# An attention layer and a routed expert layer on one core: token turning, early results and early weights in another order

## The chip, the core and the metric

The kernel runs on one core of a Trainium2 chip. The core has five engines that run at the same time, each with its own queue of instructions, taken in order: TensorE (PE in the profile; its weight loads are PEld) multiplies matrices, VectorE (DVE) and ScalarE (ACT) work elementwise, GpSimd (POOL) does the same more slowly and issues the transfers with computed addresses, and SyncE (SP) issues plain transfers. Engines wait for each other and for transfers (DMA) by semaphores. Products land in PSUM, eight banks of 128 partitions by 512 words; everything else lies in SBUF.

The metric is device time in microseconds (us) of one execution.

## The reference, cut to what matters

First a linear attention with a state per head, for 4 batches, 8 heads, 768 steps and 48 channels a head:

```
for t in range(S):
    cur   = u * k_t  (outer)  v_t
    y_t   = r_t . (state + cur)
    state = w * state + k_t (outer) v_t
```

Its output, 3072 tokens of 384 channels, goes through a layer of 8 experts, of which each token takes one:

```
logits     = x @ w_gate                     # 3072 x 8
expert_idx = argmax(logits); gate = softmax(logits)[expert_idx]
for e in range(8):
    h        = relu(x[mask_e] @ w1[e])      # 384 -> 1024
    out[mask_e] = gate * (h @ w2[e])        # 1024 -> 384
```

All is computed in 32-bit floats.

## The kernel before, in words

The order of the work is written out by hand: what stands first in the program stands first in its engine's queue, and nothing is moved by a scheduler.

**Attention in 16 turns.** A turn `i` is one batch and one pair of heads; time is cut into 6 chunks of 128 steps (`G = 6`). SP loads `rk` (keys and receptances) and `vk` (values and keys by token). VectorE scales the first by powers of the decay (`RK`, L257). In a turn TensorE runs, in this order: `p_own(i)` (L276, a token's product with itself, into bank `dsb`), `p_scores` for chunks 0 to 3 (L288, banks `X0`, `X1`), `p_ds(i)` (L311, the chunks' state products, into `dsb`), `p_tr(i - 2)` (L349, tokens of two turns ago turned so that a token is a row, together with their part of the logits, into bank `tr` and a corner of `X23`), `p_scores` for chunks 4 and 5 (`X23`), and `p_out(i - 1)` (L331 and L336, outputs of the turn before, into `yps`). In turns 6 and 10 and 14, between `p_ds` and `p_tr`, small products rank a batch's tokens within their experts (`p_rank`, L376 to L379). ScalarE builds diagonals (L294) from `own`, VectorE masks scores into them (L300, L302) and runs the states through time (`scan`, L316), ScalarE copies outputs (`out_t`, L341) and turned tokens (`keep`, L354 and L355, into `xb`). Two products into `dsb` or reads of it are ordered as if the whole bank were one thing: a product waits until VectorE has read what stood there before.

**Routing.** After a batch's last turn, VectorE finds each token's expert (`choose`), `slots` gives it a row in a table `rows` in memory, ordered by expert, and POOL sends tokens there, 128 at a time (`send`, L401, one indirect transfer per chunk). Of the batch before the last, chunk 0 goes in turn 14 and chunks 1 to 5 in turn 15.

**Experts.** Experts 0 and 1 start early: their first 160 tokens, known to be there after three batches, run as two `early` passes. Eight `late` passes follow: the rest of experts 0 and 1 (224 and 192 tokens), then the other six by size (416 down to 364), whose numbers are read by SP at run time. A pass has an inner layer `L1` (L463: for each of 8 blocks `f`, three products into one of four banks, then a ReLU on ScalarE, L465) and an outer layer (`L2`, L474, channels as rows, transposed by VectorE, scaled into `yo`; and `tokens_out`, L502, for the first 128 or 256 tokens, tokens as rows). Results go to `out` by indirect transfers on POOL (`scatter`, L520). Weights stand in two sets of buffers, `w1s` and `w2s`, each of four quarters of 384 KB; pass `k` uses set `k % 2`. SP loads them (`weights`, L420): `w1s(0)` in turn 12, `w2s(0)` in turn 13, `w1s(1)` in turn 14, `w2s(1)` in turn 15. SP also loads the passes' rows (`load`, L446), behind the sends that write them.

**Around the change.** In turn 12, `count(cnt2)` (a product with ones, L412, and a subtraction on VectorE, L413) tells if experts 0 and 1 have their 160 tokens. Early inner layers are mixed into the end of the attention: blocks 0 and 1 of the first pass, then `p_tr(14)`, `keep(14)`, `p_out(15)`, block 2, `p_tr(15)`, `keep(15)`, `choose(3)`, blocks 3 to 5, `p_rank(3)`, the sends of the last batch, and the rest. Then both early outer layers, and a check that all decays are in range: `in_range` (two VectorE instructions, L205 and L206, that make `okw`), a product with ones (L680, into `tr`), and the sum into `flag` (L681, L683). The late passes come after it. A kernel for inputs that break these assumptions (`general`) stands behind a branch on `flag` and doesn't run here.

A one-element copy on POOL into `turn` (L572 and others) computes nothing that is used: POOL waits for what it reads, and so does everything behind it.

Of the kernel before, what the change touches and what calls it, by code (L numbers as in the profile page):

```python
# [20 lines left out]
N = B * S  # L21
# [22 lines left out]
def straight(tc, rk, vk, w, w1, w2, out, flag):  # L44
# [365 lines left out]

    def count(dst):
        nc.tensor.matmul(dsb[:, 480:480 + E], lhsT=ones, rhs=osum, start=True, stop=True, skip_group_check=True)  # L412
        nc.vector.tensor_tensor(dst, dsb[:, 480:480 + E], basef, op=ALU.subtract)  # L413


    def weights(ws, w, k):

        e = late[k].e if k < E else k - E
        for q in range(4):
            nc.sync.dma_start(ws[k % 2][q], w[e, q] if isinstance(e, int) else w[ds(e, 1), q].rearrange("e p a c -> (e p) a c"))  # L420

    def weights1(k):
        weights(w1s, w1, k)

    def weights2(k):
        weights(w2s, w2, k)

    class Pass:
# [29 lines left out]
        def L1(self, fs=range(FT)):  # L458
            h = self.h
            for f in fs:  # L460
# [4 lines left out]
                nc.scalar.activation(h[:, f, 0:self.n], p[:, 0:self.n], func=ACT.Relu)  # L465

        def L2(self):
# [20 lines left out]
            for j in range(g):  # L488
                scatter(out4, ix[:, j:j + 1], yo[:, j, :], N * HP)
# [42 lines left out]
    for b in range(B - 1):  # L532
        for k, cs in enumerate(((0,), (1, 2), (3, 4), (5,)) if b < B - 2 else ((0,), (1, 2, 3, 4, 5))):
            sends[4 * b + 6 + k] = (b, cs)
# [30 lines left out]
    for i in range(1, U):  # L565
# [3 lines left out]
        p_own(i)  # L569
        own_t(i)  # L570
        if i > 1:
# [12 lines left out]
        mask(i, 1)  # L584
        p_ds(i)
# [4 lines left out]
        if 2 <= i:  # L590
            p_tr(i - 2)
# [20 lines left out]
        if i == 12:  # L612
            weights1(0)
            count(cnt2)
            nc.vector.tensor_scalar(out=viol[:, 12:14], in0=cnt2[:, 0:2], scalar1=float(EARLY), scalar2=None, op0=ALU.is_lt)
# [12 lines left out]
    p_out(U - 1)  # L628
    out_t(U - 1)
    early[0].L1(range(2, 3))  # L630
# [5 lines left out]
    early[0].L1(range(3, 6))  # L636
# [4 lines left out]
    early[0].L1(range(6, FT))  # L641
    early[1].L1()
# [14 lines left out]

    count(cnt)
# [14 lines left out]
    for p in late[2:]:  # L673
        p.e = nc.values_load(who[0:1, p.k - 2:p.k - 1], engines=[ENG.SP], min_val=2, max_val=E - 1,
                             skip_runtime_bounds_check_because="a sum over one place")
    early[0].L2()
    late[0].xT()
    early[1].L2()
    in_range()
    nc.tensor.matmul(tr[:, 496:496 + HP], lhsT=ones[0:KP], rhs=okw, start=True, stop=True, skip_group_check=True)  # L680
# [539 lines left out]
```

## Time and profile before

| | us |
|---|---|
| median of 4 runs | 390.74 |
| the four runs | 388.79, 390.67, 390.81, 391.04 |
| the profiled execution, its own time | 390.26 |
| its span, first to last instruction | 388.5 |
| TensorE busy | 374.8 |
| VectorE, ScalarE, POOL busy | 138.4, 121.2, 148.1 |
| turns of the attention | to 113.6 |
| early passes | 113.6 to 146.2 |
| late passes | from 148.1 |

The span is one execution; its own time is 1.76 us longer. Lines of the profile are read so: a group has the line of the kernel, the engine, the operation, `out<-in` by the program's tile names, shapes, how many, and then busy us and mean ns. A product of 32-bit floats is recorded twice, so eight products count x16. A wait reads "engine, what it was about to do `<-` whom it waited for: us in total, times, the longest". The chain follows the work that ended last back from the end: start, length, what. "issue" in it is time in which nothing that the profile shows was waited for. In a table of stretches, the five engines' busy time is followed by the granted TensorE clock (1.00 is full), the share of the DMA engines' time, and GB/s.

### The profile page before, as it was taken

The numbers are of one execution on the slowest core, as the hardware profiler recorded it, in microseconds if no ns is written. First come the engines' busy times: TensorE is split into PE (matmuls) and PEld (weight loads), VectorE is DVE, ScalarE is ACT, GpSimd is POOL, SyncE is SP. The second block draws the span as 40 slices with busy tenths as digits, with TensorE's granted clock in tenths as the row PEclk, the third lists the DMA queues.
The fourth block names the chain that finished last, engine by engine and source line by source line (L and its number), as shares of the span: only waits on it lengthen the run. The fifth ranks groups of instructions, "written<-read, shape, count | busy, mean of one in ns | idle before, by whom it ended". The sixth has DMA issues, their size and how long they took to land.

```text
span 388.5 us, 7741 instructions
## 1 busy us (share of the span) xinstructions
PE 374.8 (96%) x2997; PEld 285.0 (73%) x2997; DVE 138.4 (36%) x334; ACT 121.2 (31%) x348; POOL 148.1 (38%) x163
## 2 busy tenths in 40 slices
PE   6999999999999998999999999999999999999992
PEld 6788888888888997985585675585576567766761
DVE  8977796888852232030111121111102112111020
ACT  2678687877774201301202201210210120001100
POOL 3479689988851536003021034005105203342051
PEclk9999999999999998999999999999999999999997
DMA  7996886868689342859339317514823832502301
GB/s 217 286 255 212 260 251 220 273 186 270 218 255 384 132 90 76 199 164 283 101 96 250 112 62 203 154 54 146 228 82 101 225 96 86 173 19 89 117 21 46
DMA packets 34974, 65.00 MB, mean 167 GB/s; under 512 B 18378, under 2 KB 19410, under 8 KB 34928
## 3 DMA queue, kind: packets, MB, share of 16 engines
q1 hardware_dynamic: 31120, 54.58, 47.8%
q0 software_dynamic: 3808, 9.84, 7.0%
q8 instruction: 25, 0.41, 0.4%
q14 instruction: 21, 0.17, 0.1%
HBM read 53.29 MB, written 11.26 MB: 166 GB/s over the span
## 4 chain that ended last, share of the span: by engine, by line
PE 93%; issue 2%; DVE 1%; POOL 1%; ACT 0%; POOLq 0%
PE X L463 33%; PE tr L502 11%; PE yps L474 10%; PE dsb L502 8%; PE X L288 7%; PE yps L331 6%; PE dsb L474 5%; PE tr L349 4%; PE yps L336 3%; PE dsb L311 2%; PE X L349 2%; PE dsb L276 2%; POOL rp L263 0%; DVE pw L127 0%; DVE yps L68 0%
## 5 line engine op out<-in xcount | busy, mean ns | idle before, releaser
L463 PE MATMUL X<-xT,w1s 128*128 128x224 f32 (+7 forms) x384 | 115.5, 462 | 0.4 <-PE tr L680 0.4
L463 PEld LDWEIGHTS X<-xT,w1s 128*128 128x128 f32 x384 | 72.9, 194 | 43.3 <-issue 23.5
L465 ACT ACTIVATE hT<-X 128x224 f32<-128x224 f32 (+7 forms) x64 | 29.6, 462 | 203.1 <-PE X L463 203.1
L520 POOL DMA_INDIRECT out_dram<-yo,ix x33 | 32.3, 978 | 158.5 <-DVE ia L497 130.4
L294 ACT ACTIVATE A<-ident,own 128x128 f32<-128x128 f32 x192 | 57.9, 388 | 7.3 <-DVE own L280 7.3
L502 PE MATMUL tr<-w2s,hT 128*128 128x384 f32 x128 | 48.4, 487 | 0.0
L502 PE MATMUL dsb<-w2s,hT 128*128 128x384 f32 x96 | 37.7, 486 | 0.0
L401 POOL DMA_INDIRECT rows<-xb,slot x24 | 29.6, 1231 | 15.2 <-issue 6.4
L502 PEld LDWEIGHTS tr<-w2s,hT 128*128 128x128 f32 x128 | 23.8, 190 | 14.8
L474 PEld LDWEIGHTS yps<-hT,w2s 128*128 128x128 f32 x256 | 32.5, 191 | 2.0 <-issue 0.9
L474 PE MATMUL yps<-hT,w2s 128*128 128x96 f32 (+7 forms) x256 | 33.3, 283 | 0.0
L288 PE MATMUL X<-RK 48*128 48x128 f32 x384 | 30.3, 289 | 1.7 <-DVE RK L257 1.7
L476 DVE STREAM_TRANSPOSE yq<-yps 128x160 f32<-128x160 f32 (+3 forms) x16 | 5.1, 321 | 74.8 <-PE yps L474 74.8
L455 DVE STREAM_TRANSPOSE xT<-xs 128x416 f32<-128x416 f32 (+3 forms) x24 | 11.3, 521 | 53.3 <-DMA xs<-rows 53.2
L288 PEld LDWEIGHTS X<-RK 48*128 48x128 f32 x384 | 24.0, 187 | 8.5 <-issue 4.6
L257 DVE TENSOR_TENSOR RK<-rk,TT 112x1536 f32<-112x1536 f32 x16 | 27.7, 1731 | 0.0
L502 PEld LDWEIGHTS dsb<-w2s,hT 128*128 128x128 f32 x96 | 18.2, 190 | 12.7
L263 POOL TENSOR_TENSOR rp<-rk 112x768 f32<-112x768 f32 x15 | 27.3, 1818 | 0.1
L300 DVE COPY_PREDICATED A<-strict,X 128x512 f32<-128x512 int32 x32 | 22.9, 733 | 4.5 <-ACT A L294 4.4
L331 PE MATMUL yps<-A,vk 128*48 128x128 f32 x384 | 24.3, 276 | 0.0
L520 POOL DMA_INDIRECT out_dram<-yt,it x14 | 13.7, 978 | 25.0 <-DVE yt L514 23.1
L514 DVE TENSOR_SCALAR yt<-tr,xg 128x384 f32<-128x384 f32 x8 | 4.9, 618 | 51.1 <-PE tr L502 51.1
(134 smaller groups left out, 396.3 us busy)
## 6 DMA issues: line engine op xcount, KB each, us to landing
w1s<-in_w_dram SPq DMA_DIRECT2D x40, 384.0 KB, 3.1
w2s<-in_w_dram SPq DMA_DIRECT2D x32, 384.0 KB, 3.8
rk<-in_rk_dram SPq DMA_DIRECT2D x16, 672.0 KB, 6.8
vk<-in_vk_dram SPq DMA_DIRECT2D x16, 528.0 KB, 4.5
xs<-rows SPq DMA_DIRECT2D x16, 169.0 KB, 4.9
rows<-zt SPq DMA_DIRECT2D x1, 1248.0 KB, 6.7
xs<-rows SPq DMA_DIRECT2D x8, 156.0 KB, 4.3
out_dram<-yo,ix POOLq DMA_INDIRECT x33, 2.2
```

Of the source, the lines that this page charges most:

```text
L257: nc.vector.tensor_tensor(RKs[i % 3][0:KP].rearrange("p u (c t) -> p u c t", t=C), x[0:KP].rearrange("p u (c t) -> p u c t", t=C), bc(TT[: ...
L263: (eng or nc.gpsimd).tensor_tensor(rps[i % 2][0:KP], x[0:KP, 0], x[0:KP, 1], op=ALU.mult)
L288: nc.tensor.matmul(o, lhsT=r[q, 1, c * C:(c + 1) * C], rhs=r[q, 0, c * C:(c + 1) * C], start=True, stop=True, skip_group_check=True)
L294: nc.scalar.activation(A[:, place(c, h), :], ident, func=ACT.Copy, scale=own[i % 2][:, c, h:h + 1])
L331: nc.tensor.matmul(o(c, h), lhsT=v[:, c, h * D:(h + 1) * D], rhs=A[:, place(c, h), :], start=c < 2, stop=c == 0, skip_group_check=True)
L349: nc.tensor.matmul(trv[c // 4][:, c % 4, :], lhsT=yTs[i % 3][0:KP, c & 1, (c // 2) * C:(c // 2 + 1) * C], rhs=sel[:, c & 1, i % HP, :], st ...
L401: s_ = nc.gpsimd.indirect_dma_start(out=rows[:, :], out_offset=bass.IndirectOffsetOnAxis(ap=slot[b % 2][:, c:c + 1], axis=0), in_=xbs[b % ...
L463: nc.tensor.matmul(p[:, 0:self.n], lhsT=w1s[self.k % 2][f // 2][:, m, f % 2 * 128:(f % 2 + 1) * 128], rhs=self.t[:, m, 0:self.n], start=m ...
L465: nc.scalar.activation(h[:, f, 0:self.n], p[:, 0:self.n], func=ACT.Relu)
L474: nc.tensor.matmul(p[:, 0:n], lhsT=w2s[self.k % 2][f // 2][:, f % 2, m * 128:(m + 1) * 128], rhs=self.h[:, f, self.c:self.n], start=f == 0 ...
L502: nc.tensor.matmul(tbank[t][:, 0:DM], lhsT=self.h[:, f, t * 128:(t + 1) * 128], rhs=w2s[self.k % 2][f // 2][:, f % 2, :], start=f == 0, st ...
L520: s_ = nc.gpsimd.indirect_dma_start(out=to[:, :], out_offset=bass.IndirectOffsetOnAxis(ap=at, axis=0), in_=x, in_offset=None, bounds_check ...
```

## The change

- In each turn from 2 on, `p_tr(i - 2)` stands ahead of `p_ds(i)` (and of the ranks) instead of behind them.
- The product of `count` is split off as `p_count`. In turn 12 it stands right behind `p_own(12)`, with the subtraction and the comparison right behind `own_t(12)`.
- SP loads half of `w1s(0)` in turn 12 and the other half in turn 14. The loads of `w1s(1)`, `w2s(0)` and `w2s(1)` are issued by ScalarE, one quarter behind one ReLU of the early inner layers.
- Of batch 2, chunks 3 to 5 are sent after `keep(14)`, behind a copy into `turn`.
- `L2` of an early pass no longer scatters its results. Its ten transfers stand one at a time in the first three late inner layers, each behind a copy into `turn` that reads a finished block of `h`.
- `in_range` moves ahead of the first late transposes, and the check's product and sum (`okay`) behind the first late inner layer and the second late transposes.

```diff
-    def weights(ws, w, k):
+    def weights(ws, w, k, qs, eng):
...
-        for q in range(4):
-            nc.sync.dma_start(ws[k % 2][q], ...)
+        for q in qs:
+            eng.dma_start(ws[k % 2][q], ...)
...
-        def L1(self, fs=range(FT)):
+        def L1(self, fs=range(FT), then=()):
...
                 nc.scalar.activation(h[:, f, 0:self.n], p[:, 0:self.n], func=ACT.Relu)
+                if then:
+                    load, k, q = then.pop(0)
+                    load(k, (q,), nc.scalar)
...
-            for j in range(g):
-                scatter(out4, ix[:, j:j + 1], yo[:, j, :], N * HP)
+            if self.nt:
+                self.blocks_out()
+
+        def blocks_out(self, js=None):
+            for j in js or range(self.g - self.gc):
+                scatter(out4, self.ix[:, j:j + 1], self.yo[:, j, :], N * HP)
...
-        for k, cs in enumerate(((0,), (1, 2), (3, 4), (5,)) if b < B - 2 else ((0,), (1, 2, 3, 4, 5))):
+        for k, cs in enumerate(((0,), (1, 2), (3, 4), (5,)) if b < B - 2 else ((0,), (1, 2))):
...
         p_own(i)
+        if i == 12:
+            p_count()
         own_t(i)
+        if i == 12:
+            count(cnt2)
+            nc.vector.tensor_scalar(out=viol[:, 12:14], ...)
...
+        if 2 <= i:
+            p_tr(i - 2)
         p_ds(i)
         if rt:
             p_rank(b)
             slots(b)
         scan(i)
-        if 2 <= i:
-            p_tr(i - 2)
...
         if i == 12:
-            weights1(0)
-            count(cnt2)
-            nc.vector.tensor_scalar(out=viol[:, 12:14], ...)
+            weights1(0, (0, 1))
         if i == 13:
             for p in early:
                 p.load()
-            weights2(0)
         if i == 14:
-            weights1(1)
-        if i == 15:
-            weights2(1)
+            weights1(0, (2, 3))
 
-    early[0].L1(range(0, 2))
+    early[0].L1(range(0, 2), [(weights1, 1, 0), (weights1, 1, 1)])
     p_tr(U - 2)
     keep(U - 2)
+    nc.gpsimd.tensor_copy(turn, xbs[1][0:1, G - 1, 2, 0:1])
+    send(B - 2, range(3, G))
     p_out(U - 1)
     out_t(U - 1)
-    early[0].L1(range(2, 3))
+    early[0].L1(range(2, 3), [(weights1, 1, 2)])
...
-    early[0].L1(range(3, 6))
+    early[0].L1(range(3, 6), [(weights1, 1, 3), (weights2, 0, 0), (weights2, 0, 1)])
...
-    early[0].L1(range(6, FT))
-    early[1].L1()
+    early[0].L1(range(6, FT), [(weights2, 0, 2), (weights2, 0, 3)])
+    early[1].L1(range(0, 2))
+    early[1].L1(range(2, FT), [(weights2, 1, q) for q in range(4)])
...
+    p_count()
     count(cnt)
...
+    def okay():
+        nc.tensor.matmul(tr[:, 496:496 + HP], lhsT=ones[0:KP], rhs=okw, ...)
+        nc.vector.tensor_scalar(out=viol[:, E:E + HP], ...)
+        nc.vector.tensor_reduce(flag, viol[0:1, 0:E + HP + 2], axis=AX, op=ALU.add)
+
     early[0].L2()
+    in_range()
     late[0].xT()
     early[1].L2()
-    in_range()
-    nc.tensor.matmul(tr[:, 496:496 + HP], lhsT=ones[0:KP], rhs=okw, ...)
-    nc.vector.tensor_scalar(out=viol[:, E:E + HP], ...)
-    nc.vector.tensor_reduce(flag, viol[0:1, 0:E + HP + 2], axis=AX, op=ALU.add)
     n = len(late)
+    waiting = [(x, j) for x in early for j in range(ge)]
...
-            p.L1()
+            for f in range(FT):
+                p.L1((f,))
+                if (k < 2 and f % 2 or k == 2 and f % 4 == 1) and waiting:
+                    nc.gpsimd.tensor_copy(turn, p.h[0:1, f, 0:1])
+                    x, j = waiting.pop(0)
+                    x.blocks_out((j,))
             late[k + 1].xT()
+            if k == 0:
+                okay()
```

More of the change, by code (lines that the diff above doesn't have):

```diff
@@ L409, in ids, with p_count, weights1, weights2 @@
                        channel_multiplier=4)
+    def p_count():
+        nc.tensor.matmul(dsb[:, 480:480 + E], lhsT=ones, rhs=osum, start=True, stop=True, skip_group_check=True)
     def count(dst):
-        nc.tensor.matmul(dsb[:, 480:480 + E], lhsT=ones, rhs=osum, start=True, stop=True, skip_group_check=True)
         nc.vector.tensor_tensor(dst, dsb[:, 480:480 + E], basef, op=ALU.subtract)
-    def weights(ws, w, k):
+    def weights(ws, w, k, qs, eng):
         e = late[k].e if k < E else k - E
-        for q in range(4):
[L420 to L426, printed above, removed]
+        for q in qs:
+            eng.dma_start(ws[k % 2][q], w[e, q] if isinstance(e, int) else w[ds(e, 1), q].rearrange("e p a c -> (e p) a c"))
+    def weights1(k, qs=range(4), eng=nc.sync):
+        weights(w1s, w1, k, qs, eng)
+    def weights2(k, qs=range(4), eng=nc.sync):
+        weights(w2s, w2, k, qs, eng)
     class Pass:
@@ L456, in xT @@
                                     self.x[:, 0:self.g, 32 * m:32 * m + 32])
-        def L1(self, fs=range(FT)):
-            h = self.h
+        def L1(self, fs=range(FT), then=()):
+            h, then = self.h, list(then)
             for f in fs:
@@ L569, in straight @@
         p_own(i)
+        if i == 12:
+            p_count()
         own_t(i)
+        if i == 12:
+            count(cnt2)
+            nc.vector.tensor_scalar(out=viol[:, 12:14], in0=cnt2[:, 0:2], scalar1=float(EARLY), scalar2=None, op0=ALU.is_lt)
         if i > 1:
@@ L612, in straight @@
         if i == 12:
-            weights1(0)
-            count(cnt2)
-            nc.vector.tensor_scalar(out=viol[:, 12:14], in0=cnt2[:, 0:2], scalar1=float(EARLY), scalar2=None, op0=ALU.is_lt)
+            weights1(0, (0, 1))
         if i == 13:
@@ L675, in straight @@
                              skip_runtime_bounds_check_because="a sum over one place")
+    def okay():
+        nc.tensor.matmul(tr[:, 496:496 + HP], lhsT=ones[0:KP], rhs=okw, start=True, stop=True, skip_group_check=True)
+        nc.vector.tensor_scalar(out=viol[:, E:E + HP], in0=tr[:, 496:496 + HP], scalar1=KP - 0.5, scalar2=None, op0=ALU.is_lt)
+        with nc.allow_low_precision("whole numbers"):
+            nc.vector.tensor_reduce(flag, viol[0:1, 0:E + HP + 2], axis=AX, op=ALU.add)
     early[0].L2()
+    in_range()
     late[0].xT()
     early[1].L2()
-    in_range()
-    nc.tensor.matmul(tr[:, 496:496 + HP], lhsT=ones[0:KP], rhs=okw, start=True, stop=True, skip_group_check=True)
-    nc.vector.tensor_scalar(out=viol[:, E:E + HP], in0=tr[:, 496:496 + HP], scalar1=KP - 0.5, scalar2=None, op0=ALU.is_lt)
-    with nc.allow_low_precision("whole numbers"):
-        nc.vector.tensor_reduce(flag, viol[0:1, 0:E + HP + 2], axis=AX, op=ALU.add)
     n = len(late)
+    waiting = [(x, j) for x in early for j in range(ge)]
     for k, p in enumerate(late):
```

## The prediction

> **What bounds the kernel now.** I read the page first, then the waits of TensorE, the chain around every place where TensorE waits, and the clock there. The page's busy row says which engine to follow:
>
> ```profile
> PE 374.8 (96%) x2997; PEld 285.0 (73%) x2997; DVE 138.4 (36%) x334; ACT 121.2 (31%) x348; POOL 148.1 (38%) x163
> ```
>
> TensorE has work for 374.8 of 388.5 us, and its work is the same after the change, so time can come only from its idle places, from its clock, and from the order of its instructions. The waits name every idle place:
>
> ```profile
> PE X L288 <- DVE RK L257: 1.7, 1, 1.7
> ...
> PE X L107 <- POOL ident masks.py:199: 1.4, 1, 1.4
> ...
> PE tr L680 <- DVE okw L206: 1.4, 1, 1.4
> ...
> PE X L463 <- ACT xb L355: 0.4, 1, 0.4
> PE dsb L276 <- POOL rp L263: 0.4, 1, 0.4
> PE X L463 <- PE tr L680: 0.4, 1, 0.4
> PE dsb L276 <- DVE cnt L413: 0.4, 1, 0.4
> ```
>
> RK, ident and rp lie in the first 16 us, which the change leaves alone. Three places remain: 93.5 us (cnt), 121.5 us (xb), and the largest, where the early experts' outer layer ends and the late inner layers begin. The chain there, start and length in us:
>
> ```profile
> 143.98 2.19 PE yps L474 x16
> ...
> 146.59 0.64 DVE yoe L487
> ...
> 147.34 0.17 DVE okw L206
> ...
> 147.56 0.18 PE tr L680
> 147.74 0.35 issue
> 148.09 2.05 PE X L463 x7
> ```
>
> A tiny product (L680, the check on the decay's range) needs okw, which VectorE makes only after the second early expert's results. From 146.17 to 148.09 the array does almost nothing. The stretches that follow show a second bill; the column after the five engines' busy times is the granted clock:
>
> ```profile
> 145.60:149.00 3.40, 1.63 (x11) 1.29 (x10) 2.46 (x10) 0.00 (x0) 2.39 (x4) 1.00 0.09 29
> 149.00:152.40 3.40, 3.40 (x11) 3.08 (x10) 0.03 (x1) 0.71 (x2) 2.72 (x3) 0.50 0.12 43
> 152.40:156.00 3.60, 3.60 (x20) 3.60 (x20) 0.00 (x0) 0.99 (x3) 0.98 (x1) 0.99 0.51 160
> ```
>
> After 3.4 us in which TensorE worked only 1.63, its clock was halved for 3.4 us.
>
> **The change part by part.** *The range check.* in_range goes ahead of the first late transposes, and the L680 product behind the first late inner layer. Between L474's end and the first late L463 nothing is left: its input xT was transposed at 140.65 to 141.65, some 4.5 us early, and in_range (two instructions of 0.16) takes 0.3 of that. Gain: 148.09 - 146.17 = 1.92. The product is now paid in the middle of inner layers. Its nearest row is the other such product, L412, with 0.01 in the chain; the far end is its present 0.53 (147.56 to 148.09). I take 0.1, nearer to L412, since okw is by then long made. VectorE's answer to it queues behind the second late transposes and holds up only flag, read at the end.
>
> *The clock.* 3.4 us at half speed lose 1.7. By length: the late inner layers of width 224 and 192 took 18.80 us (148.09 to 166.89), while the one of width 416, as many columns, took 16.76 (177.41 to 194.17), a difference of 2.04, of which some is the overhead of 48 more records. I take 1.8, ends 0 (the halving comes all the same) and 2.0.
>
> [...]
>
> *The early count* (p_count, count at turn 12). Before, the next own-product waited 0.35 for cnt on VectorE (chain: L412 at 93.34, L276 at 93.81). Now the product follows p_own(12), and its 0.17 us subtraction runs beside 1.1 us of scores and 1.5 us of token turning before anything else writes dsb. Gain 0.34. On VectorE scale(13) starts some 0.35 later; RK is needed only in the next turn, over 4 us on. ScalarE's diagonals move by about 0.1, and ScalarE idles more than that in each turn.
>
> *Token turning ahead of the state products*, 14 turns. One turn before:
>
> ```profile
> 107.52 1.16 PE L288 MATMUL X<-RK 48*128 48x128 f32 x16
> 108.61 0.65 PE L311 MATMUL dsb<-vk,Kd 128*48 128x48 f32 x20
> 109.19 1.14 PE L349 MATMUL tr<-sel,yT 112*128 112x104 f32 x8
> 110.71 0.71 PE L288 MATMUL X<-RK 48*128 48x128 f32 x8
> ```
>
> By starts: scores 1.09, state products 0.58, turning 1.52, no idle. In turn 1, which has no turning, scores follow the state products at the same 0.58 (17.23 to 17.81). Near 115.36 the turning takes 1.42 ahead of L331. So the order is worth between -0.1 and +0.1 a turn, 1.4 either way in all; I take 0, because 0.58 repeats whatever follows. The state products move from 108.61 to about 110.1 and end where the turning did, at 110.71; the scan that reads them began at 111.32, behind the second mask, so it doesn't move. In turns with ranks, slots likewise waits behind masks (rko at 104.93; ranks would end near 104.2). Nor does the turning lack its input: yT was copied by 107.87, and it starts at 108.6.
>
> *Weights from ScalarE's queue.* The twelve loads of w1s(1), w2s(0), w2s(1) left SP between 107.89 and 116.30; half of w1s(0) takes their place. Now each goes out after an activation of the early inner layers. As TensorE needs f every 0.82 us and an activation takes 0.30, 0.5 us is free for an issue. Issues and landings of all sixteen before:
>
> ```profile
> L420 SPq DMA_DIRECT2D w1s<-in_w_dram x8: 430/501/1255, 92.9 to 111.3; - x8
> L420 SPq DMA_DIRECT2D w2s<-in_w_dram x8: 328/474/1318, 107.9 to 116.0; - x8
> ...
> DMA to landing us min/median/max: 3.8/9.0/11.7
> ```
>
> The median issue just fits. Before the first product of each weight there is: w1s(1) last quarter, issued about 123.4, needed at 131.2 (126.25 plus six f): 7.8 us. w2s(0) last quarter, 127.65, needed at 134.5: 6.9. w2s(1) first, 129.3, needed at 139.5: over 10. The 9.0 median would miss two of these, but it belongs to a burst of twelve loads in 8.4 us, at 396 GB/s and a DMA share of 1.02 (114 to 122 us). Spread, loads (4.7 MB) and nine sends (1.9 MB) make 6.6 MB from 115 to 136 us, 16 to 17 of 21 us at that rate; so I take 4 to 6 us, near the minimum, and no stall. One place is tight: the issue between the third activation (ends 120.47) and keep (121.05), which ends the 0.42 wait at 121.5. With 0.5 it just passes, with 1.32 it costs 0.7; I take 0.1.
>
> [...]
>
> *Sends and early results.* Three sends of batch 2 wait for keep(14) and go at about 117.4 to 121.1 instead of 112.7 to 117.6, before POOL's ids at 122.42. The last batch's sends must land before the late rows load (135.19, landing in 2.1 to 2.4); these are needed by 145, so 3 to 4 us later is still free. The ten early scatters (0.98 us each on POOL, 140.99 to 153.6) move beside the late inner layers, each behind a tiny POOL copy that waits for an activation. Behind them in POOL's order stand the late scatters, the first near 174; nothing on TensorE waits for an early scatter, and activations that reuse an h wait for a copy two passes old. Cost 0, ends 0 and 0.3 at the most, as TensorE shows no idle from 148.09 to 381.
>
> **Sum.** 1.92 - 0.1 + 1.8 + 0.34 - 0.1 = 3.9. The profiled execution took 390.26 (span 388.5 and 1.76 around it), so 386.4, span 384.6. It stands 0.5 below the median of the four runs, 390.74, which would give 386.9; I say 386.5.
>
> **Rivals.**
> *The clock's 1.8 is not won* (the halving is tied to something else): 388.3. For it: the idle 1.69 at 7.5 us shows no halving. Against: only this idle stretch fills half of 3.4 us, and the halving follows at once.
> *Half-late weights*: at 9.0 us, w1s(1)'s last quarter lands at 132.4 and w2s(0)'s at 136.65, stalling 1.2 and, since the first stall shifts the need, 1.0 more: 388.6.
> *Slower, weights late for good*: at the 11.7 us maximum they land at 135.1 and 139.35, stalls of 3.9 and 1.0, and such an idle stretch would halve the clock again, 1.7: 386.4 + 6.6 = 393.0. It decides from about 10 us on, a first stall of 2.2 with the clock's 1.7 eating the 3.9. Against it is the missing burst.
> *The turn's order*: 14 x 0.1 lost, 387.8, or gained, 385.0.
>
> **How the numbers follow.** Forecast 0.63 (own range 385.6 to 387.4); clock not won 0.08; half-late weights 0.10; slower 0.06; order lost 0.07; order gained 0.06. Up to 388.5 the range holds all but the slower case and part of two others, so 385.2 to 388.5. A measurement tells 0.5% (1.95 us) from no change: under 388.8 lies everything but the slower case and the upper parts of the second and third, so faster 0.86, same 0.09, slower 0.05.
>
> **What would show it.** Right: no TensorE wait on okw or cnt; the first late inner layer at about 145.9 directly behind L474; the two late inner layers in about 16.9 us; granted clock 1.00 until the end; turns still 6.55 us. Wrong: TensorE waiting for w1s or w2s between 124 and 140, activations lagging behind queue issues on ScalarE, a stretch of clock 0.5 elsewhere, or turns off 6.55.

## The result, and the profile after

The changed kernel took 386.75 us (median of 38 executions, 386.53 to 389.37); the kernel before, run beside it, 390.52 (median of 59, 388.40 to 393.78). The ratio is 0.9923, with a 95% interval of 0.9906 to 0.9939: faster by 0.6 to 0.9%. The medians stand 3.8 us apart, the means (387.58 and 390.61) 3.0, and the ratio lies by the means: the times of both kernels fall into groups, which are told below. The forecast was 386.5, the range 385.2 to 388.5.

The page of the changed kernel (387.4 us of span, 389.28 us of time) has the same work on TensorE, and nearly no idle place left. First its busy row, then all waits of TensorE that are named; in the second view the columns are the time waited in total, how often, and the longest.

```profile
PE 375.4 (97%) x2997; PEld 285.8 (74%) x2997; DVE 138.2 (36%) x334; ACT 121.1 (31%) x348; POOL 148.9 (38%) x174
```

```profile
PE X L288 <- DVE RK L257: 2.2, 1, 2.2
PE X L107 <- POOL ident masks.py:199: 1.4, 1, 1.4
PE X L466 <- ACT xb L355: 0.4, 1, 0.4
PE dsb L276 <- DVE rp L263: 0.2, 1, 0.2
```

Lines have moved: the inner layers' products are now L466 (L463 before), their activations L468 (L465), the outer layers' L480 (L474), the range check's product L692 (L680), the weight loads L422 (L420); L276, L288, L311, L349 stand where they stood. The waits for okw and for cnt are gone, the 0.4 for xb is as it was. The chain of the same execution at the place of the first, start and length in us:

```profile
146.30 2.17 PE yps L480 x16
148.48 9.08 PE X L466 x48
157.56 0.01 PE tr L692
157.56 7.91 PE X L466 x48
165.47 1.76 PE yps L480 x16
```

The late inner layers begin where the early outer layer ends, the check's product costs 0.01 between the two, and from the first late inner product to the first late outer one it is 16.99 us (148.31 to 165.31) in place of 18.64 (148.09 to 166.73): the granted clock is 1.00 in the one stretch and 0.91 in the other.

This execution shows something else, though, which the forecast had not foreseen. In the table of stretches, taken from one record of the clock to the next (TensorE, weight load, VectorE, ScalarE, POOL, granted clock, DMA share, GB/s) the clock is halved at the start, for twice 3.41 us:

```profile
7.98:11.39 3.41, 1.95 (x25) 1.25 (x25) 3.12 (x5) 0.38 (x2) 0.00 (x0) 1.00 1.00 270
11.39:14.80 3.41, 3.41 (x38) 2.60 (x35) 3.41 (x5) 3.41 (x13) 1.12 (x2) 0.50 1.03 257
14.80:18.22 3.42, 3.42 (x16) 3.22 (x16) 1.28 (x3) 0.25 (x1) 1.99 (x2) 0.50 1.05 292
```

It makes the stretch from the first to the second own product 8.18 us long, where the kernel before has 5.63. Among the 38 times, 25 lie between 386.5 and 387.7 and 13 between 389.0 and 389.4, a distance of 2.5: the profiled execution is one of the 13, which lie above the range. The kernel before waits for RK at its start too (1.7 us; here 2.2). So the two profiled executions of the first comparison can't simply be subtracted; the experiments below bring a pair that can.

### The profile page after: what moved, and what is told of

The parts are those of the page before. It is cut to its first block, busy times and chain, and to the rows that moved or that the text cites. A ratio compares the mean times of both kernels' runs of the same rounds, so it can differ in the third digit from the quotient of the medians.

```text
span 387.4 us, 7759 instructions
## 1 busy us (share of the span) xinstructions
PE 375.4 (97%) x2997; PEld 285.8 (74%) x2997; DVE 138.2 (36%) x334; ACT 121.1 (31%) x348; POOL 148.9 (38%) x174
## 4 chain that ended last, share of the span: by engine, by line
PE 95%; DVE 3%; issue 0%; ACT 0%; POOL 0%; POOLq 0%
PE X L466 33%; PE tr L512 11%; PE yps L480 10%; PE dsb L512 8%; PE X L288 7%; PE yps L331 6%; PE dsb L480 5%; PE tr L349 4%; PE yps L336 3%; PE dsb L311 3%; PE X L349 2%; PE dsb L276 2%; PE yps L107 1%; DVE TT L146 1%; DVE RK L257 0%; DVE pw L127 0%
## 5 line engine op out<-in xcount | busy, mean ns | idle before, releaser
L466 PE MATMUL X<-xT,w1s 128*128 128x224 f32 (+7 forms) x384 | 113.9, 457 | 0.0
L466 PEld LDWEIGHTS X<-xT,w1s 128*128 128x128 f32 x384 | 71.6, 190 | 40.9 <-issue 21.0
L468 ACT ACTIVATE hT<-X 128x224 f32<-128x224 f32 (+7 forms) x64 | 29.5, 461 | 199.4 <-PE X L466 198.7
L480 PEld LDWEIGHTS yps<-hT,w2s 128*128 128x128 f32 x256 | 32.5, 191 | 2.0 <-issue 0.9
L480 PE MATMUL yps<-hT,w2s 128*128 128x96 f32 (+7 forms) x256 | 33.3, 284 | 0.0
L288 PE MATMUL X<-RK 48*128 48x128 f32 x384 | 30.9, 293 | 2.2 <-DVE RK L257 2.2
L288 PEld LDWEIGHTS X<-RK 48*128 48x128 f32 x384 | 24.4, 190 | 7.9 <-issue 4.6
L401 POOL DMA_INDIRECT rows<-xb,slot x24 | 24.1, 1003 | 15.5 <-issue 7.0
L263 POOL TENSOR_TENSOR rp<-rk 112x768 f32<-112x768 f32 x15 | 29.4, 1958 | 0.1
```

The costliest lines, as they stand in the source:

```text
L263: (eng or nc.gpsimd).tensor_tensor(rps[i % 2][0:KP], x[0:KP, 0], x[0:KP, 1], op=ALU.mult)
L288: nc.tensor.matmul(o, lhsT=r[q, 1, c * C:(c + 1) * C], rhs=r[q, 0, c * C:(c + 1) * C], start=True, stop=True, skip_group_check=True)
L401: s_ = nc.gpsimd.indirect_dma_start(out=rows[:, :], out_offset=bass.IndirectOffsetOnAxis(ap=slot[b % 2][:, c:c + 1], axis=0), in_=xbs[b % ...
L466: nc.tensor.matmul(p[:, 0:self.n], lhsT=w1s[self.k % 2][f // 2][:, m, f % 2 * 128:(f % 2 + 1) * 128], rhs=self.t[:, m, 0:self.n], start=m ...
L480: nc.tensor.matmul(p[:, 0:n], lhsT=w2s[self.k % 2][f // 2][:, f % 2, m * 128:(m + 1) * 128], rhs=self.h[:, f, self.c:self.n], start=f == 0 ...
```

## The experiments

My theory was the sum on record: a gap behind the early outer layers (1.9), a clock halved by it (1.8), a wait for the count (0.34), and nothing from the rest. The rivals were that the clock's part comes from elsewhere, and that the other parts (turning order, weights from ScalarE's queue, early results later) are worth something after all.

The first eight kernels ran on two chips on which the kernel before took 406.92 us (17 runs, 401.16 to 410.52) and 404.99 us (11 runs, 401.69 to 411.11), some 15 more than at first. So a ratio of these eight isn't to be compared with 0.9923; what I read from them is the length of stages, which can be compared, and why these chips are slower, which is told at the end. The changed kernel itself was not run on those two chips. The last four kernels ran on a third chip, where the kernel before took 390.82 us.

**One part alone, and one part back: the range check**

To the kernel before, only this part:

```diff
     early[0].L2()
+    in_range()
     late[0].xT()
     early[1].L2()
-    in_range()
-    (product with ones, comparison, sum into flag)
 ...
             late[k + 1].xT()
+            if k == 0:
+                okay()      # the same three
```

> The kernel before with the range check alone moved (in_range ahead of the first late transposes, its product behind the first late inner layer). Theory (the wait on okw and the clock that it halves are nearly the whole gain): no TensorE wait on okw, the two late inner layers in 16.9 to 17.0 us instead of 18.8, and times in two groups, near 386.7 and 389.3, so a median some 3 us under before. Rival (the gain needs the weights or the early results out of the way): TensorE waits for something else between 140 and 150 us and the time falls by less than 1.5 us.

To the changed kernel, this part undone:

```diff
     early[0].L2()
-    in_range()
     late[0].xT()
     early[1].L2()
+    in_range()
+    okay()
 ...
-            if k == 0:
-                okay()
```

> The changed kernel with the range check back where it was. Theory: nearly all is given back: TensorE waits 1.4 us for okw again, the shortest times stand near 388.2 (386.6 and 1.9 less 0.3), the two late inner layers take 18.8 us in runs with the halved clock; median within 0.6 us of before. Rival (several parts share the gain): median at least 1.5 us under before.

By the stage: from the first product of the early outer layers to the first late inner product is 15.22 us in the kernel before (132.87 to 148.09). With the check alone moved it is 13.12 (143.63 to 156.75), in the changed kernel 13.12 (135.19 to 148.31), and with the check back 15.23 (141.94 to 157.17). So the gap is worth 2.10 us, the same by itself and put back, and the pair on the third chip below gives it too. The times were 401.49 us (397.44 to 403.19; ratio 0.986, interval 0.980 to 0.992) for the check alone and 396.23 (394.68 to 398.28; ratio 0.972, 0.967 to 0.977) for the check back. The second was expected within 0.6 us of the kernel before and is 10.7 below it: the sign that was put down for the rival, that several parts share the gain. On the slower chips other parts do have a price of their own, as the parts undone one by one show further down.

The clock is another matter. With the check back, the gap came back and the halving did not. Two stretches of that kernel, cut where the clock's records begin and end:

```profile
155.41:158.82 3.41, 1.81 (x10) 1.68 (x10) 2.36 (x10) 0.11 (x1) 0.00 (x0) 1.00 0.00 0
158.82:162.23 3.41, 3.41 (x20) 3.41 (x19) 0.00 (x0) 1.20 (x4) 1.15 (x2) 1.00 0.37 112
```

TensorE's idle 1.41 us before the product and 0.36 behind it fell so that 1.60 of them lay in the first of these stretches, with 1.81 of work; the clock stayed at 1.00. My forecast had tied the halving to the gap; the gap alone doesn't bring it. Nor does the time worked in such a stretch alone decide: in the same execution, at the early inner layers, one with 1.83 of work had a halving behind it:

```profile
117.87:121.28 3.41, 1.83 (x15) 1.50 (x14) 0.00 (x0) 1.26 (x4) 0.90 (x1) 1.00 0.51 168
121.28:124.69 3.41, 3.41 (x29) 2.87 (x27) 0.00 (x0) 0.84 (x2) 1.25 (x3) 0.50 0.53 192
```

**The gap filled, in the kernel before**

```diff
     in_range()
+    p_fill(6, X01[1][:, 0, :])
     (product with ones into tr)
```

> The kernel before with six idle products (the fill that it has at its start, 0.22 us each) ahead of the range check's product, in the time in which TensorE waits for okw. They compute nothing that is used. The wait for okw stays, only the idleness goes. Theory (the halved clock comes from the idle stretch): the two late inner layers take 16.9 us instead of 18.8 though they start no earlier (about 148.1), and the two upper groups of before's times (near 390.4 and 392.8) are gone. Rival (the halving is tied to something else there): still 18.8 us in most runs, time as before.

It took 406.1 us (400.47 to 413.72), ratio 1.0005 (0.995 to 1.006), and doesn't answer its question. The fill delayed what it was to cover: VectorE's transposes of the last early results began at 159.93, behind the end of the filling products (159.20), so the check's product still waited 2.1 us, behind the fill (159.20 to 161.30), and the clock was halved behind it:

```profile
159.59:163.01 3.42, 1.34 (x7) 1.21 (x7) 2.50 (x10) 0.00 (x0) 1.46 (x2) 1.00 0.04 14
163.01:166.42 3.41, 3.41 (x11) 3.07 (x10) 0.00 (x0) 0.71 (x2) 2.50 (x4) 0.50 0.08 29
```

What it does give is one more halving behind a stretch in which TensorE worked 1.34 of 3.42 us.

**The start filled, in the changed kernel**

```diff
-    p_fill(17, X01[1][:, 0, :])
+    p_fill(25, X01[1][:, 0, :])
```

> The changed kernel with 25 instead of 17 idle products at the start, while VectorE makes the first scaled keys. Theory (the profiled run of the changed kernel was 2.6 us longer because TensorE's idle 2.2 us at 7 us halved its clock from 11.4 to 18.2): the idle place shrinks to under 0.6 us, no run shows the halved clock there, all times lie near 386.6, and the group near 389.2 is gone. Rival (the two groups have another cause): 389.2 still shows in about a third of the runs; or the fill delays the first scores and all times rise by up to 0.5.

394.04 us (392.77 to 398.71), ratio 0.966 (0.960 to 0.972). The wait for RK at 7 us is gone and so is the halving behind it: the clock is 1.00 from 6.8 to 140.0 us, and the first own product to the second takes 5.46. The times tell nothing of the two groups on this chip, and this is one execution: that the fill removes the halving for good isn't shown by it. A halving at another place, behind a wait of 2.9 us that the executions on the third chip don't have, again follows a stretch with little work, 1.42 us:

```profile
136.54:139.95 3.41, 1.42 (x10) 1.38 (x11) 0.23 (x2) 0.90 (x3) 0.39 (x1) 1.00 1.01 405
139.95:143.37 3.42, 3.42 (x15) 3.42 (x14) 1.71 (x10) 0.01 (x1) 0.00 (x0) 0.50 0.61 203
```

**The other four parts, each undone in the changed kernel**

The turning behind the state products again:

```diff
-        if 2 <= i:
-            p_tr(i - 2)
         p_ds(i)
 ...
         scan(i)
+        if 2 <= i:
+            p_tr(i - 2)
```

> The changed kernel with the older tokens' turning back behind the state products. Theory (the order is worth nothing, as its blocks take the same time either way): turns without ranks 6.55 us as before, the three turns with ranks shorter by 0.1 (6.73 against 6.82), time within 0.4 us of the changed kernel's. Rival (the new order hides a wait): a TensorE wait for own or keys appears in some turn and the time rises by over 0.5 us.

The early weights from SP's queue again:

```diff
-            weights1(0, (0, 1))
+            weights1(0)
         if i == 13:
 ...
+            weights2(0)
         if i == 14:
-            weights1(0, (2, 3))
+            weights1(1)
+        if i == 15:
+            weights2(1)
 ...
-    early[0].L1(range(0, 2), [(weights1, 1, 0), (weights1, 1, 1)])
+    early[0].L1(range(0, 2))
     (and so at the other calls)
```

> The changed kernel with all early weights back in SyncE's queue, where they were. Theory (neither queue lets TensorE wait): time within 0.3 us of the changed kernel's; the last batch's sends land sooner, so the late rows are loaded some 3 us earlier, and TensorE doesn't notice. Rival (the saturated transfers of 114 to 122 us cost something once the check is out of the way): slower by 0.5 us or more.

The early results sent out at once again:

```diff
-            if self.nt:
-                self.blocks_out()
+            self.blocks_out()
 ...
-    waiting = [(x, j) for x in early for j in range(ge)]
+    waiting = []
```

> The changed kernel with the ten early scatters back in the early outer layers. Theory: POOL issues them at about 141 to 154 us again and nothing on TensorE changes; time within 0.3 us. Rival (ten transfers beside the late loads of rows delay the first late transposes, whose slack fell to 2.5 us): TensorE waits for xT near 146 and the time rises by 0.5 us or more.

The early count at the end of turn 12 again:

```diff
         p_own(i)
-        if i == 12:
-            p_count()
         own_t(i)
-        if i == 12:
-            count(cnt2)
-            (comparison into viol)
 ...
             weights1(0, (0, 1))
+            p_count()
+            count(cnt2)
+            (comparison into viol)
```

> The changed kernel with the early count back at the end of turn 12. Theory: TensorE waits 0.35 us for cnt again, turn 12 takes 7.1 us instead of 6.7, time up by 0.35. Rival (the wait was hidden by something): no change, under 0.1.

| undone | us (lowest, highest) | ratio to before, 95% | turns 8, 9, 10 | turns 12, 13, 14 | early inner layers |
|---|---|---|---|---|---|
| turning order | 397.32 (396.39, 399.79) | 0.984 (0.980, 0.988) | 7.47, 7.50, 7.14 | 7.26, 7.64, 7.10 | 23.75 |
| weights | 391.34 (390.03, 392.74) | 0.968 (0.964, 0.972) | 6.55, 6.55, 6.81 | 6.66, 6.77, 7.16 | 22.72 |
| early results | 394.68 (393.33, 397.76) | 0.977 (0.972, 0.982) | 6.57, 6.55, 6.81 | 6.66, 6.85, 7.13 | 25.31 |
| early count | 396.57 (393.55, 402.22) | 0.978 (0.972, 0.984) | 6.56, 6.55, 6.81 | 8.26, 6.55, 6.81 | 22.32 |

A turn is counted from the start of its own product to that of the next; the last column goes from the first early inner product to the first early outer one. From the early outer layers on, all four are alike: 13.12 or 13.13 us to the first late inner product, and 231.39 or 231.40 from there to TensorE's last product. So the early results cost the late passes nothing, sent out at once or one at a time. With the turning behind the state products, turns 8 and 9 are 0.9 us longer, 10 and 12 by 0.3 and 0.6, 13 by 0.8 to 1.1; with the count at its old place, turn 12 is 1.6 longer. On the chip of the first profiles the order was worth nothing in a plain turn but turn 3 (6.67 to 6.55) and the count 0.4, so both have a price on this chip that they don't have there. The weights have no plain reading: the early inner layers differ among these kernels by up to 3 us, in waits that come and go (and 1.7 of the 25.31 is a halved clock), and the kernel with SP's weights has 22.72, between two with ScalarE's.

**Both kernels and two variants on the third chip**

The last four ran side by side on a chip on which the kernel before took 390.82 us (17 runs): both kernels unaltered, and the changed kernel with small edits meant to be better still.

> The changed kernel unaltered, on the chip on which the kernel before is run beside it. My theory (the check's gap 1.9 to 2.1 us, the clock 1.7 only where the window of 3.4 us falls so, the count 0.4; and on a chip where TensorE's signals reach the other engines late, 0.85 us in each of several turns through the turning order and up to 2.9 us through the count): if the kernel before stands at 388 to 394 us here, this one is 2 to 5 us shorter (ratio 0.987 to 0.995) and its plain turns take 6.55 us; if the kernel before stands above 400 us, this one is 8 to 13 us shorter (ratio 0.967 to 0.98), with turns 8 to 10 at 6.55. Rival, that on such a chip everything is stretched in the same proportion and the parts of the change have the value that they have elsewhere: 3 to 5 us shorter also there (ratio 0.988 to 0.993). In either case 13.1 us from the first outer product of the first early expert to the first late inner layer.

> The kernel before unaltered, for its profile on the same chip as the others. My theory: ratio 1.0 within 0.5%; 15.2 us from the first outer product of the first early expert to the first late inner layer, with the wait of 1.9 us for okw in it, whatever the chip. On a chip where it takes over 400 us, turns 8 to 10 take 7.1 to 7.5 us each in place of 6.55, with waits between the own product and the state product, and turn 12 over 8 us; on a chip where it takes 388 to 394 us all plain turns are 6.55. Rival, stretched throughout: all turns longer by the same 3 to 4%.

The changed kernel: 386.73 us (386.56 to 386.82), ratio 0.9886 (0.985 to 0.992). The kernel before, as one of the four: 391.74 (388.61 to 392.97), ratio to itself 1.001 (0.998 to 1.005). Here neither profiled execution has a halved clock at its start, so they can be subtracted: 390.68 and 386.73 us, 3.95 between them. This execution of the kernel before has a halved clock behind the check, and not all of its executions have. Of the 29 on this chip, 9 have a mean granted clock of 0.989 to 0.991, as it has, and take 390.2 to 391.4 us; 10 have 0.993 to 0.996, as the changed kernel's six have (0.993 to 0.997), and take 388.5 to 389.9; 10 have 0.982 and take 392.7 to 393.0, which fits a start at half clock on top. So in about a third of its executions the kernel before has the gap and not the halving. The profiled kernel before, chain and stretches:

```profile
144.24 2.19 PE yps L474 x16
...
147.61 0.17 DVE okw L206
147.78 0.04 issue
147.82 0.18 PE tr L680
148.00 0.35 issue
148.35 18.80 PE X L463 x96
```

```profile
145.25:148.66 3.41, 1.64 (x12) 1.30 (x11) 1.86 (x8) 0.00 (x0) 2.70 (x3) 1.00 0.14 43
148.66:152.08 3.42, 3.42 (x11) 3.10 (x10) 0.64 (x3) 0.36 (x1) 2.50 (x4) 0.50 0.12 43
```

The changed kernel's chain there:

```profile
143.77 2.17 PE yps L480 x16
145.94 9.08 PE X L466 x48
155.02 0.01 PE tr L692
155.03 7.91 PE X L466 x48
```

And the count in turn 12, first the chain of the kernel before, then that of the changed one:

```profile
93.61 0.12 PE dsb L412
93.73 0.02 issue
93.76 0.18 DVE cnt L413
93.94 0.14 issue
94.07 0.51 PE dsb L276 x8
```

```profile
86.91 0.44 PE dsb L276 x8
87.35 0.11 PE dsb L412
87.46 1.09 PE X L288 x16
```

Before, the next own product waited for VectorE's answer; now the count's product is followed by scores at once.

The two variants were these, the second with the weights from SP's queue on top:

```diff
-    p_fill(17, X01[1][:, 0, :])
+    p_fill(25, X01[1][:, 0, :])
 ...
-        if 2 <= i:
+        if 2 <= i and not rt:
             p_tr(i - 2)
         p_ds(i)
 ...
         scan(i)
+        if 2 <= i and rt:
+            p_tr(i - 2)
 ...
-    early[0].L1(range(3, 6), [...])
+    early[0].L1((4, 3, 5), [...])
```

> The changed kernel with three small edits: 25 filling products in place of 17 at the start (they compute nothing that is used), the turning behind the state products again in the three turns with ranks alone, and the fifth inner block ahead of the fourth where the fourth waits 0.42 us for the copies of the turned tokens. My theory: no idle stretch at 7 us and so no halved clock there (2.55 us in the executions that had it), 0.3 from the turns with ranks, 0.4 from the block order: 0.7 us below the changed kernel where the clock falls well for both, 3.2 where only the changed kernel's clock is halved, so a median 0.7 to 2 us below it (ratio to the kernel before 0.002 to 0.005 lower). [...]

> The same three edits, and the early weights from SyncE's queue as in the kernel before. If issuing from ScalarE's queue costs time (the theory for a chip where the stage from the first early inner layer to the first early outer layer took 23.8 to 25.4 us with it and 22.7 without): 1 to 3 us below the kernel with the three edits alone on such a chip. If the issues run beside the activations at no cost (as in the changed kernel's profile, 0.33 us each beside activations of 0.30): within 0.3 us of it, stage 19.3 us in both.

They took 387.27 us (386.70 to 387.98; ratio 0.990, 0.987 to 0.994) and 387.10 (386.71 to 387.45; ratio 0.990, 0.986 to 0.993): neither beats the changed kernel, and the 0.7 us expected of the first didn't come. Its time is 0.5 above the changed kernel's, and no halved clock is seen that would explain it: in the profiled execution (386.70 us) the clock is 1.00 to TensorE's last product. Two of its three edits did what they were to do and found nothing to gain or gave little. None of the changed kernel's six executions here shows the 389 us of a halved start, so there was nothing for the fill to save, and whether it prevents that start isn't shown; the three turns with ranks went from 6.81 each to 6.74, 6.72 and 6.72, 0.25 in all. The third failed: with block 4 ahead of block 3, TensorE's wait for xb was replaced by a longer one. In the list of TensorE's waits the first line is of the changed kernel, the second of the variant:

```profile
PE X L466 <- ACT xb L355: 0.4, 1, 0.4
```

```profile
PE X L466 <- ACT hTe L468: 0.6, 1, 0.6
```

TensorE ran blocks 4 and 3 at once (120.84 to 122.65) and then stood until ScalarE had done their activations, which it began only at 122.62, behind the exponential of the last batch's softmax. TensorE's last product ends at 377.14 us in the variant and 377.17 in the changed kernel; why the times stand 0.5 apart (387.27 against 386.73) the profile doesn't say, and with six executions each I leave that open. The weights from one queue or the other make no difference here: 19.3 us from the first early inner product to the first early outer one with SP, 19.4 with ScalarE, 19.2 in the changed kernel.

## Why the prediction was right

Right in sign, in size, and in most of its terms. The median lies in the range with some luck, though: the halved start, which the prediction left out because the change doesn't touch the first 16 us, puts 13 of the 38 executions above 388.5, and had it come in most of them the median would have been 389.2. Of the signs of being right, "granted clock 1.00 until the end" failed in the first profiled execution. The sum, from the pair on the third chip (stages from start to start, so that the two spans' beginnings don't enter):

| step | on record | measured | from |
|---|---|---|---|
| gap at the check | 1.92 | 2.10 | 15.23 to 13.12 us, first early outer product to first late inner one |
| clock | 1.8 | 1.65 | 233.04 to 231.40, from there to TensorE's last product; the check's product is in it |
| check's product put elsewhere | -0.1 | about 0 | 0.01 in the chain |
| early count | 0.34 | 0.42 | turn 12: 7.08 to 6.66 |
| turning order, plain turns | 0 | 0.38 | turn 3: 6.93 to 6.55; the others alike |
| turning order, turns with ranks | 0 | -0.25 | 6.74, 6.72, 6.72 to 6.81 each |
| ScalarE's issue ahead of keep | -0.1 | 0 | wait for xb 0.42 in both |
| weights, sends | 0 | 0 | 19.24 to 19.23, the early inner layers |
| early results | 0 | 0 | late passes as long with them sent at once |
| sum | 3.9 | 4.3 | times 3.95 apart, 390.68 and 386.73 |

TensorE's last product ends 4.23 us earlier (the changed kernel's first turn starts 0.07 later), and 0.2 of that is given back behind the last product, where 7.57 us follow before and 7.78 after; the prediction had put nothing there.

*Where the sum was off, its terms were mis-sized.* The gap and the count are each larger than the idle time that I read (2.10 for 1.92, 0.42 for 0.35), because idle time between records leaves out that, where TensorE doesn't stop, the next product begins before the last one's recorded end: by 0.16 us at the late inner layers of the changed kernel (145.78, where the chain has the outer layer's end at 145.94). The lengths of stages from start to start have it. The clock's term was 0.15 too large.

*The turning order was taken as 0 with 1.4 either way.* It is 0 in plain turns, as the repeated 0.58 said, except in turn 3. There, in the old order, the state products take 0.97 us to the next start (0.70 in the first execution), in the new one, with the turning ahead of them, 0.59; what holds them up the profile doesn't name, but with the turning alone put back, on a slower chip, turn 3 again takes 6.67. The new order loses 0.08 in each turn with ranks, where I had looked at slots and masks and not at TensorE itself; these turns come back to 6.74, 6.72 and 6.72 in the variant that puts the turning behind in them, whose other edits lie outside these turns. So the gain and the loss nearly cancel, and the 0 is right in sum and not in its parts.

*The clock: the size was right, the condition was not.* I put down 1.8 with an end at 0 for a halving that comes all the same, and the rival "clock not won" at 0.08 for a halving tied to something else; against it I held that only this idle stretch fills half of 3.4 us. What the runs show is a third thing: the halving at this place needs the gap, but comes only in some of the executions that have it. Of the four profiled executions with the gap three have a halving behind it (1.65 us in the pair), the check put back has none; of the ten without the gap none has one from the end of the early outer layers to TensorE's last product. These are stretches of 3.41 us that bear on the condition, each cut by the clock's own records:

| kernel | stretch, from | work in the stretch | clock in the next |
|---|---|---|---|
| gap filled | check, 159.59 | 1.34 | 0.50 |
| start filled | early inner layers, 136.54 | 1.42 | 0.50 |
| before, both executions | check, 145.61 and 145.25 | 1.64 and 1.64 | 0.50 |
| check alone moved | start, 6.28 | 1.65 | 1.00 |
| check back | check, 155.41 | 1.81 | 1.00 |
| turning back | early inner layers, 137.16 | 1.82 | 1.00 |
| check back | early inner layers, 117.87 | 1.83 | 0.50 |
| early results back | early inner layers, 137.85 | 1.99 | 1.00 |
| early results back | early inner layers, 124.20 | 2.02 | 0.50 |
| check alone moved | early inner layers, 118.92 | 2.12 | 0.50 |
| gap filled | early inner layers, 118.63 | 2.25 | 0.50 |

Of the full stretches at clock 1.00 in all the traces, up to TensorE's last product, those with up to 1.64 us of work have a halving behind them each time, those between 1.65 and 2.53 (a halved start, with the check back) in some cases and not in others, those above that never. So "less than half of 3.41 worked" isn't the rule, and what decides in between is open. The line for the turning back:

```profile
137.16:140.57 3.41, 1.82 (x12) 1.58 (x12) 0.00 (x0) 0.30 (x1) 2.07 (x3) 1.00 1.03 403
```

The clock's records begin at different places of the kernel's work from one execution to the next: in the two profiled ones of the kernel before that of the halved clock begins at 149.02 and at 148.66 us. Before had the halving in some executions and not in others, going by the mean clocks above, which is a part of its wide spread (388.4 to 393.8). That the place of these records decides whether the halving comes, as I put down for the changed kernel's second run, is my estimate; no run shows it. The change takes gap and halving away together. The forecast's 1.8 is right for an execution with the halving, such as the one that it was subtracted from (390.26); beside the executions of the third chip without it (median 389.2) the changed kernel's 386.73 is 2.5 us shorter.

In the profiles of the first comparison every full stretch between two records of the clock is a whole number of 3.41 us: 143.36, 3.41 and 232.11 us (42, 1 and 68 times 3.413) in the kernel before, 6.83, 6.83 and 365.23 (2, 2 and 107 times) in the changed one. A stretch with 1.77 us of idle time was followed by a halved clock in the two executions of the kernel before (1.64 of 3.41 worked); with the check back, 1.60 us of idle time in one was not.

*Weights from ScalarE's queue: the estimate held, but for the last two loads.* I took 4 to 6 us of flight in place of the 9.0 in a burst. In the changed kernel on the third chip (issues of the weights, with least, median and most time of an issue in ns; then their flight in us):

```profile
L422 ACTq DMA_DIRECT2D w2s<-in_w_dram x8: 334/334/335, 123.6 to 131.2; - x8
...
L422 ACTq DMA_DIRECT2D w1s<-in_w_dram x4: 334/334/382, 114.5 to 122.8; - x4
...
DMA to landing us min/median/max: 3.1/5.4/7.6
```

In the first profile of the changed kernel it was 3.1, 3.7 and 6.3. On the third chip the last two quarters of w2s(1) took 7.0 and 7.6. The nearest call was the last of them, issued at 131.20 and landed at 138.78, 2.1 us before the first product that reads it, at 140.89; the last quarter of w2s(0) landed at 131.84 and was read from 134.37. No product waited for weights, so neither of the two rivals with late weights came. The 0.1 for the issue ahead of keep was not paid, since the issue, 0.33 us from 119.97, ran beside an activation of 0.30 from 119.96. The stretch of ScalarE's timeline at that place:

```profile
119.96 0.30 ACT L468 ACTIVATE hTe<-X 128x160 f32<-128x160 f32 x1 [0.27 <-PE X L466]
119.97 0.33 ACTq L422 DMA_DIRECT2D w1s<-in_w_dram  x1
```

*The sends' cover was used.* I had named 3 to 4 us by which the late rows could come later at no cost. On the third chip they were transposed at 142.50 to 143.50 and needed at 145.78, 2.3 us, where before it was 4.5: no stall, but half of the cover is gone.

## What to carry to other kernels

Read a gap's worth from start to start of the stages around it, not from the idle time between records, and add to it the clock that it may cost in the 3.4 us behind it (1.65 us here), as a chance and not as a certainty: the kernel before paid it in about two of three executions on the third chip. Look how much of one stretch of 3.41 us the gap can empty: with 1.77 of it idle the clock behind was halved in both profiles of the kernel before, with 1.60 idle, with the check back, it was not. Where an engine's answer stands in TensorE's queue (okw, cnt), put work that needs no answer between the question and the next use; for the count that was worth 0.42 us. An edit that is worth next to nothing where the signal is raised 0.04 us behind the product's end can be worth microseconds where it comes 1.40 behind it, as the turning order was: 0.9 us in each of turns 8 and 9; a part that costs nothing and separates a question from its use is worth keeping.

## What was not expected of the hardware

**A start that is halved in some executions.** The 2.5 us between the two groups of times come from the two halved stretches behind the wait for RK (8.18 against 5.63 us from the first own product to the second); the changed kernel's executions above 389.0 us have a mean granted clock of 0.986 or 0.987, the others 0.989 to 0.997. Here busy time alone doesn't decide: the changed kernel worked 1.95 us in the stretch before the halving and 1.94 in one at the same place on the third chip that had none behind it:

```profile
6.25:9.67 3.42, 1.94 (x20) 1.75 (x20) 3.33 (x4) 0.00 (x0) 0.00 (x0) 1.00 1.04 288
9.67:13.08 3.41, 3.16 (x52) 2.13 (x52) 3.11 (x5) 1.99 (x8) 0.00 (x0) 1.00 1.04 291
```

Nor does a busy stretch end it: in the changed kernel's first profile TensorE is busy for all 3.41 us from 11.39 to 14.80, and the clock is halved for 3.42 more. What else counts there, the kind of products or the stretch before, isn't settled. On the third chip none of the changed kernel's six executions has the halved start, and 10 of the 29 of the kernel before have the clock and the time that fit it, so the change isn't seen to bring it.

**Chips on which TensorE's signals come late.** On the two slower chips the same program is not stretched throughout. Its plain turns take 6.55 us there too, its late passes 231.4 to 231.6 us from the first inner product to TensorE's last where the clock is not halved, as on the third chip. What is longer stands at a few places, and at these another engine begins late on what TensorE has finished. The kernel before with the check alone moved, on a slower chip, in turn 8, TensorE's timeline and VectorE's (start, length, what, in brackets the idle time before):

```profile
61.38 0.51 PE L276 MATMUL dsb<-rp,wug 112*2 112x192 f32 x8
61.82 1.16 PE L288 MATMUL X<-RK 48*128 48x128 f32 x16
63.82 0.66 PE L311 MATMUL dsb<-vk,Kd 128*48 128x48 f32 x20 [0.84 <-issue]
```

```profile
63.38 0.38 DVE L280 STREAM_TRANSPOSE own<-dsb 128x192 f32<-128x192 f32 x1 [2.89 <-PE X L288]
```

and the kernel before on the third chip:

```profile
60.62 0.51 PE L276 MATMUL dsb<-rp,wug 112*2 112x192 f32 x8
```

```profile
61.26 0.38 DVE L280 STREAM_TRANSPOSE own<-dsb 128x192 f32<-128x192 f32 x1 [1.54 <-PE dsb L276]
```

VectorE copies the own product 0.13 us after its end on the one (60.62 + 0.51 to 61.26) and 1.49 after it on the other (61.38 + 0.51 to 63.38), and TensorE then stands 0.84 us at the state products, which write the bank that is being copied. The traces also hold the times at which the semaphore that VectorE waits on was raised. The raise that ended this wait is at 63.29 on the slower chip, 1.40 us behind the product's end, and at 61.16 on the third, 0.04 behind it. VectorE starts 0.1 us after it on both, so it is the signal that is late and not VectorE. It comes back at the same places: turns 8, 9 and 10 take 7.46, 7.47 and 7.14 us in this kernel, 7.47, 7.51 and 7.14 in the one with the gap filled, and 7.47, 7.50 and 7.14 with the turning back on the other slower chip, where the third chip has 6.55, 6.55 and 6.72.

With the turning ahead of the state products this wait is covered: the turning needs no answer from VectorE, and with it turns 8 and 9 take 6.55 again. So the change's order, which on the third chip gained 0.38 us in turn 3 and nothing in the other plain turns, saves 0.9 us in each of the plain turns among them. The count's place is the same story at a larger size; in the same kernel's list of TensorE's waits:

```profile
PE dsb L276 <- DVE cnt L413: 2.1, 1, 2.1
```

where the third chip has 0.3. This is a part of how the variants of the changed kernel came to be 8 to 14 us below the kernel before there (ratios 0.966 to 0.984), more than the 4 us of the sum: in this trace turns 8, 9, 10 and 12 (7.46, 7.47, 7.14 and 9.43) take 4.9 us more than in the changed kernel. The rest isn't accounted for; neither of the two kernels was profiled unaltered there, and the early inner layers take 21.9 to 25.4 us on these chips in place of 19.2. Why signals are late on those chips, and always at the same turns, is open: no run here tells neighbours on the chip, the supply of instructions or something else apart. Whether ScalarE's queue costs anything there is open too; the kernel with SP's weights was the shortest of its four (391.34 us), but the early inner stage of one with ScalarE's was shorter still (22.3 us against 22.7).
